# Staging tiles, the start of later attention and the order of the first loads in a fused attention, FFN and expert kernel

## The chip, the cores and the metric

The kernel runs on one core of one Trainium2 chip. Times are device microseconds of one launch, from the first to the last instruction and what lies around them. Engines are named as in the profile: PE (TensorE), DVE (VectorE), ACT (ScalarE), POOL (GpSimd), SP (SyncE, which here issues nearly all DMAs).

## What is computed

Three stages in a row, all in float32 at the interface:

```python
# 1. gated linear attention: 4 batches, 8 heads, 768 steps, head size 48
f = 1.0 / (1.0 + np.exp(-f_logit))
for t in range(S):
    state = f[:, :, t, :, None] * state + np.einsum('bhd,bhe->bhde', k[:, :, t], v[:, :, t])
    y[:, :, t] = np.einsum('bhd,bhde->bhe', q[:, :, t], state)
# 2. FFN over 3072 tokens: 384 -> 2048 -> 384
h = x @ w_in
x = (np.maximum(h, 0.0) + alpha * np.minimum(h, 0.0)) @ w_out
# 3. 8 experts with a capacity of 384 tokens each, filled greedily by the largest logit
logits = x @ w_gate
out[mask] = np.maximum(x[mask] @ w1[e], 0.0) @ w2[e]      # for each expert e
```

## The kernel before

The 3072 tokens are 24 chunks of 128; three chunks are a block, so there are eight blocks. Attention works chunk by chunk (`chunk`, steps `s1` to `s5`): `s1` runs two scans of 128x516 on DVE, a reciprocal and a minimum; `s2` multiplies keys and queries by the decays (two 128x512 products); `s3` makes scores on PE and masks them on DVE (two operations); `s4` and `s4s` make the output and the new state; `s5` halves the output into two parts for the FFN. All FFN matmuls have float32 operands, cut into a high and a low half, three matmuls in place of one.

The FFN weights come as pairs of 32-bit words (64-bit floats) and must be turned into such halves first: 16 chunks of 128 hidden columns, two chunks to a group `g`, eight groups. `load_w` issues four DMAs of a group (two of the first matrix, two of the second), `narrow` turns the words into floats (two ACT and two DVE instructions on 128x384 for each of 32 half chunks), `split` makes the halves (one ACT copy, one subtraction on DVE or POOL), and `gate` multiplies the second matrix by the gate on PE, so that logits come out of the FFN as eight more columns (three transposes, an ACT copy, three small matmuls, a small ACT copy and a small DVE subtraction per chunk). The result of `narrow` stands in a tile `a` of 128x384; there are three such buffers (lines 651, 666, 795, 805), so a new half chunk can be begun when an older one has been split and, for the second matrix, transposed for the gate.

`ffn1` runs one block: for each of 16 hidden chunks nine matmuls into one of two PSUM banks (`hidden`), a negative part, a combination on DVE (`SCALAR_TENSOR_TENSOR common`) and a split, and two chunks later nine matmuls into three output banks (`project`). At its end DVE copies the logits of the three chunks (`COPY lg`). In the traces and lists below, `MATMUL bank<-rounded,weights 128x384` is a hidden one and `bank<-weights,rounded 128x392` a projecting one; `weights14` and so on are the prepared weights, an even number for the first matrix of group 7, an odd one for the second.

The order of the work on each engine is made when the program is built: every operation is recorded with a priority, and `Plan.schedule` places them one by one, the one that by its costs can start first, ties by priority. It knows buffers, banks and dependencies; `behind(ops)` lets an operation start only after given ones have started. Where PE would stand idle and a bank is free, it puts in matmuls of ones (L1651). The engines then run these lists in order.

In `record`, the order around the change is: two chunk loads, attention of block 0, the weights (priority 15.5), then for b = 0 to 6 attention of block b+1 (priority 10b+10, 14 for block 1), and FFN of block b. The first loads on SP are chained by the string `FIRST` (c: a chunk's keys, queries, gates and values; w: a group of weights). A chunk's load is issued two chunks ahead into one of two buffers. `prepared` is the last operation of the weights; in the kernel before only the conversion of the expert weights (`convert`) waits for it.

Of the kernel before, what the change touches and what calls it, by code (L numbers as in the profile page):

```python
# [9 lines left out]
F32 = mybir.dt.float32  # L10
F32R = mybir.dt.float32r
BF = mybir.dt.bfloat16
I32 = mybir.dt.int32
# [7 lines left out]
N, DM, DF = B * S, H * D, 2048  # L21
# [8 lines left out]
KD = DM // 128  # L30
# [37 lines left out]
PLACES = 4  # L68
FILL = 2.0

FIRST = "c0 c1 w0 c2 w1 c3 w2 w3 c4 w4 w5 c5 w6 w7"
LOADS = 2


# [541 lines left out]
class Kernel:  # L616
# [28 lines left out]
    def constants(self, cp):  # L645
        nc = self.nc
        self.cp = cp
        self.ones = cp.tile([128, 128], BF, name="ones")
        with self.at(-4.0):
            nc.vector.memset(self.ones, 1.0)  # L650
        jp = self.sp.tile([128, 128], F32, name="a", bufs=3)
        nc.gpsimd.iota(jp, pattern=[[1, 128]], base=0, channel_multiplier=-1,
                       allow_small_or_imprecise_dtypes=True)
        self.ident = cp.tile([128, 128], F32, name="ident")
        nc.vector.tensor_scalar(self.ident, jp, 0.0, None, op0=OP.is_equal)
        self.mask = cp.tile([128, 128], BF, name="mask")
        nc.vector.tensor_scalar(self.mask, jp, 0.0, None, op0=OP.is_ge)
        self.tri = cp.tile([128, 128], BF, name="tri")
        nc.vector.tensor_scalar(self.tri, jp, 0.0, -1.0, op0=OP.is_le, op1=OP.mult)
        self.pick = cp.tile([2 * E, E], F32, name="pick")  # L660
        nc.vector.tensor_tensor(self.pick, self.ident[:2 * E, :E], self.ident[:2 * E, E:2 * E], OP.add)

        self.pairs = cp.tile([128, 128], F32, name="pairs")
        self.turn = cp.tile([128, 2], F32, name="turn")
        with self.at(PAIRS):
            two = self.sp.tile([128, 128], F32, name="a", bufs=3)
            nc.gpsimd.iota(two, pattern=[[2, 128]], base=0, channel_multiplier=-1, allow_small_or_imprecise_dtypes=True)
            nc.vector.tensor_scalar(self.pairs, two, 0.0, None, op0=OP.is_equal)
            nc.vector.tensor_reduce(self.turn[:, 0:1], self.pairs, axis=AX.X, op=OP.add)
            nc.vector.tensor_scalar(two, two, -1.0, None, op0=OP.is_equal)  # L670
            nc.vector.tensor_reduce(self.turn[:, 1:2], two, axis=AX.X, op=OP.add)
            nc.vector.tensor_add(self.pairs, self.pairs, two)
        self.eye8 = cp.tile([E, E], BF, name="eye8")
        nc.vector.tensor_copy(self.eye8, self.ident[:E, :E])

        self.cols = cp.tile([128, 128, 2], BF, name="cols")
        nc.gpsimd.iota(self.cols, pattern=[[1, 128], [0, 2]], base=0, channel_multiplier=0,
                       allow_small_or_imprecise_dtypes=True)
        nc.vector.tensor_scalar(self.cols, self.cols, -HALF, None, op0=OP.add)

        self.ok = cp.tile([WAYS + 1, 1], BF, name="ok1")
        nc.vector.memset(self.ok, -WAYS / 2.0)


        self.okl = cp.tile([WAYS + 2, E], BF, name="okl")
        nc.gpsimd.iota(self.okl[WAYS:], pattern=[[-1, E]], base=0, channel_multiplier=0, allow_small_or_imprecise_dtypes=True)
        nc.vector.tensor_scalar(self.okl[WAYS:], self.okl[WAYS:], 2.0 ** -13, None, op0=OP.mult)
        nc.vector.memset(self.okl[WAYS:WAYS + 1], -WAYS / 2.0 - 0.5)
        self.wts = cp.tile([128, E], F32, name="wts")
        nc.gpsimd.iota(self.wts, pattern=[[-1, E]], base=E, channel_multiplier=0,  # L690
                       allow_small_or_imprecise_dtypes=True)
        self.wtb = cp.tile([128, E], BF, name="wtb")
        nc.vector.tensor_copy(self.wtb, self.wts)
        self.jpv = cp.tile([128, NT, 2], F32, name="jpv")
        nc.gpsimd.iota(self.jpv[:, :, 0], pattern=[[1, NT]], base=0, channel_multiplier=0,
                       allow_small_or_imprecise_dtypes=True)
        nc.gpsimd.iota(self.jpv[:, :, 1], pattern=[[0, NT]], base=0, channel_multiplier=1,
                       allow_small_or_imprecise_dtypes=True)
        self.lg = cp.tile([128, NT, E], F32, name="lg")
        self.pmin = cp.tile([128, HP], F32, name="state")  # L700
        nc.vector.memset(self.pmin, 1.0)
# [89 lines left out]
    def prepare_in(self, g):  # L791

        a = []
        for u in range(2):
            a.append(self.sp.tile([128, KD, 128], I32, name="a", bufs=3))
            self.narrow(a[u], self.rin[:, u], self.nc.scalar)
        for u in range(2):
            f = 2 * g + u
            self.split(self.in_part(0, f), self.in_part(1, f), a[u].bitcast(F32))

    def prepare_out(self, g):

        a = []
        for u in range(2):
            a.append(self.sp.tile([128, DM], I32, name="a", bufs=3))
            self.narrow(a[u], self.rout[:, u], self.nc.scalar)
        for u in range(2):
            f = 2 * g + u
            self.split(self.out_part(0, f)[:, :DM], self.out_part(1, f)[:, :DM], a[u].bitcast(F32))
        for u in range(2):  # L810
            self.gate(2 * g + u, a[u].bitcast(F32))
# [846 lines left out]
    def record(self, cp):  # L1658
# [7 lines left out]
        def store(blk):  # L1666
            def put(t, r, logits):
                j = blk * BT + t
                (nc.sync if logits is not None else nc.scalar).dma_start(self.x2d[j * 128:(j + 1) * 128], r)
                if logits is not None:  # L1670
                    nc.vector.tensor_copy(self.lg[:, j, :], logits)
            return put
# [20 lines left out]
        def load(i):  # L1693
            self.load(i)
            loads["c", i] = self.last(3 if i else 5)

        def attend(b):
            with self.at(10.0 * b if b != 1 else ATT1):
                for i in range(b * BT, (b + 1) * BT):
                    self.chunk(i)  # L1700
                    if i + LOADS < NT:
                        with self.at(10.0 * b - 1):
                            load(i + LOADS)
# [17 lines left out]
        prepared = self.last(1)  # L1721
        self.slack = SLACK
        for b in range(NB - 1):
            attend(b + 1)
            if b == 0:
                steps = [loads[x[0], int(x[1:])] for x in FIRST.split()]
                self.plan.follow(steps)
            self.urgent = 10.0 * b + URG
            with self.at(10.0 * b + FFN):
                self.ffn1(self.xT.pop(b), store(b))  # L1730
# [95 lines left out]
```

## Time and profile before

| what | value |
| --- | --- |
| median of 3 runs | 872.51 us (870.24 to 876.36) |
| the profiled execution | 872.57 us |
| its span, first to last instruction | 870.6 us |
| PE busy | 829.7 us, 95% of the span |
| DVE busy | 580.2 us, 67% |
| ACT busy | 350.9 us, 40% |
| POOL busy | 118.6 us, 14% |
| mean granted TensorE clock | 0.979 |

The span falls into parts with different limits: up to about 147 us weights are prepared while attention and the FFN of the first block run; then FFN blocks and attention until about 534 us; then the choice of tokens and the eight experts. Shares of busy time over the whole span say little about the first part, so it is read by itself, in stretches and instruction by instruction. Busy PE time includes matmuls of ones and matmuls at the lower clock.

### The profile page before, as it was taken

To read this page: it belongs to the slowest core of one execution; us is meant where nothing else is said; L and a number is where in the kernel's file an instruction comes from. 1 tells how busy PE (TensorE), PEld (TensorE's weight loads), DVE (VectorE), ACT (ScalarE), POOL (GpSimd) and SP (SyncE) were. 2 spreads that over 40 slices of the span, in tenths; PEclk is the share of its full clock that TensorE was granted. 3 is DMA by queue.
4 is the path that set the end of the run, shared out by engine and by line. 5 is a ranking of instruction groups with operands and counts; after the bars stand their busy time and mean duration, and the time that the engine had idled before them with its cause. 6 is when DMAs were issued, how large, how long until landed. Compare 5 with 4: busy or idle time off the path is not lost. (4 is left out here: it accounts for less than half of the span.)

```text
span 870.6 us, 16049 instructions
## 1 busy us (share of the span) xinstructions
PE 829.7 (95%) x6125; PEld 764.4 (88%) x6125; DVE 580.2 (67%) x1302; ACT 350.9 (40%) x742; POOL 118.6 (14%) x111
## 2 busy tenths in 40 slices
PE   6999899999999999999999999998799999999995
PEld 4677788999999999999999998986688998999995
DVE  6998996956966966966976644655677568553220
ACT  3456775455455455455554433510112222212220
POOL 3100321200300200200300100000203203202211
PEclk7999998999999999999999999999899999999998
DMA  8996112888798698688778710007467865777400
GB/s 173 277 278 146 28 28 76 203 294 279 197 298 274 143 303 285 177 297 274 231 266 271 244 64 28 1 10 308 151 261 301 313 245 180 274 275 251 165 28 31
DMA packets 92790, 172.60 MB, mean 198 GB/s; under 512 B 31672, under 2 KB 61376, under 8 KB 92704
## 3 DMA queue, kind: packets, MB, share of 16 engines
q1 hardware_dynamic: 89056, 161.45, 58.3%
q0 software_dynamic: 3072, 9.44, 3.1%
q8 instruction: 50, 0.82, 0.4%
q10 hardware_dynamic: 576, 0.60, 0.2%
q14 instruction: 36, 0.29, 0.1%
HBM read 111.69 MB, written 59.77 MB: 197 GB/s over the span
## 5 line engine op out<-in xcount | busy, mean ns | idle before, releaser
L206 PE MATMUL bank<-rounded,weights 128*128 128x384 f32 (+1 forms) x1740 | 356.7, 346 | 2.8 <-POOL weights L206 1.6
L206 PE MATMUL bank<-weights,rounded 128*128 128x392 f32 (+1 forms) x1620 | 326.7, 346 | 3.5 <-DVE weights L206 1.9
L206 PEld LDWEIGHTS bank<-rounded,weights 128*128 128x128 f32 (+1 forms) x1740 | 306.0, 189 | 10.6 <-issue 3.7
L206 PEld LDWEIGHTS bank<-weights,rounded 128*128 128x128 f32 x1620 | 289.0, 189 | 6.9 <-DVE weights L206 3.3
L206 ACT ACTIVATE rounded<-bank 128x384 fp32r<-128x384 f32 x110 | 53.8, 491 | 198.1 <-PE bank L206 188.3
L206 DVE TENSOR_TENSOR early<-early 128x384 fp32r<-128x384 f32 (+2 forms) x196 | 117.5, 621 | 18.2 <-ACT early L206 17.0
L206 PEld LDWEIGHTS bank<-early 128*64 128x64 f32 (+2 forms) x1696 | 99.0, 154 | 19.1 <-issue 9.2
L206 PE MATMUL bank<-early 128*64 128x128 f32 (+3 forms) x1696 | 111.7, 271 | 1.0 <-ACT early L206 0.5
L206 DVE SCALAR_TENSOR_TENSOR common<-common,rest,bank 128x384 f32<-128x384 f32 x128 | 77.9, 609 | 49.4 <-ACT common L226 48.9
L206 ACT ACTIVATE early<-early 128x384 fp32r<-128x384 f32 (+2 forms) x177 | 95.3, 546 | 37.1 <-DMA wd<-early 22.4
L206 POOL TENSOR_TENSOR rounded<-common,rounded 128x384 fp32r<-128x384 f32 x40 | 52.6, 1315 | 366.3 <-ACT rounded L206 308.5
L226 ACT ACTIVATE common<-bank 128x384 f32<-128x384 f32 x128 | 62.5, 488 | 83.1 <-PE bank L206 82.3
L206 ACT ACTIVATE rounded<-common 128x384 fp32r<-128x384 f32 x118 | 61.7, 523 | 65.7 <-DVE common L206 65.5
L206 DVE TENSOR_TENSOR_SCAN early<-early 128x516 f32<-128x516 f32 x48 | 64.2, 1337 | 2.3 <-ACT early L206 1.2
L206 DVE SCALAR_TENSOR_TENSOR rounded<-bank,rounded 128x384 fp32r<-128x384 f32 x62 | 34.3, 554 | 46.4 <-ACT rounded L206 44.0
L206 DVE TENSOR_TENSOR rounded<-common,rounded 128x384 fp32r<-128x384 f32 x78 | 44.3, 569 | 27.8 <-ACT rounded L206 22.5
L206 ACT ACTIVATE common<-bank 128x384 f32<-128x384 f32 x48 | 23.3, 491 | 72.8 <-PE bank L206 69.3
L206 POOL DMA_INDIRECT out_dram<-common,late x24 | 25.5, 1062 | 171.3 <-ACT common L206 137.4
L206 POOL DMA_INDIRECT common<-x2d,late x24 | 26.8, 1118 | 150.8 <-DMA weights<-wd 119.5
L206 DVE TENSOR_TENSOR late<-late,cols 128x1536 bf16<-128x1536 bf16 (+3 forms) x53 | 42.7, 821 | 1.0
L206 DVE TENSOR_TENSOR early<-bank,mask 128x512 f32<-128x512 f32 x48 | 30.9, 684 | 6.1 <-PE bank L206 6.0
L206 DVE TENSOR_TENSOR rounded<-bank,rounded 128x384 fp32r<-128x384 f32 x48 | 26.3, 553 | 12.9 <-ACT rounded L206 12.4
(110 smaller groups left out, 494.8 us busy)
## 6 DMA issues: line engine op xcount, KB each, us to landing
wd<-early SPq DMA_DIRECT2D x128, 384.0 KB, 3.3
weights<-wd SPq DMA_DIRECT2D x64, 768.0 KB, 5.4
early<-in_w_dram SPq DMA_DIRECT2D x64, 384.0 KB, 4.3
early<-in_fkq_dram SPq DMA_DIRECT2D x46, 288.0 KB, 4.9
raw<-in_w_in_dram SPq DMA_DIRECT2D x16, 384.0 KB, 6.8
raw<-in_w_out_dram SPq DMA_DIRECT2D x16, 384.0 KB, 8.0
early<-in_v_dram SPq DMA_DIRECT2D x24, 192.0 KB, 4.9
x2d<-common SPq DMA_DIRECT2D x21, 192.0 KB, 3.0
```

The costliest lines, as they stand in the source:

```text
L206: op = self.add(engines, lambda e, b: getattr(e, method)(*[b(x) for x in a], **{n: b(x) for n, x in k.items()}), outs, ins)
L226: return e.activation(b(out), b(x), AF.Relu, scale=-1.0)
```

## The change

The staging tile `a` gets six buffers in place of three. Attention of blocks 2 to 7, with the chunk loads in it, starts only after the last operation of the weights has started (block 1 doesn't wait). The first loads stand in another order: w2, w4 and w6 go ahead of c3, c4 and c5.

```diff
-FIRST = "c0 c1 w0 c2 w1 c3 w2 w3 c4 w4 w5 c5 w6 w7"
+FIRST = "c0 c1 w0 c2 w1 w2 c3 w3 w4 c4 w5 w6 c5 w7"
+STAGE = 6
...
-        jp = self.sp.tile([128, 128], F32, name="a", bufs=3)
+        jp = self.sp.tile([128, 128], F32, name="a", bufs=STAGE)
...
-            a.append(self.sp.tile([128, KD, 128], I32, name="a", bufs=3))
+            a.append(self.sp.tile([128, KD, 128], I32, name="a", bufs=STAGE))
...
-            a.append(self.sp.tile([128, DM], I32, name="a", bufs=3))
+            a.append(self.sp.tile([128, DM], I32, name="a", bufs=STAGE))
...
         for b in range(NB - 1):
-            attend(b + 1)
+            with self.behind(prepared if b else ()):
+                attend(b + 1)
```

What this does to the lists of the engines is shown at three places.

DVE before, in the middle of the preparation, while groups 4 and 5 are narrowed (`raw_142`, `raw_138`, `raw_134`) and split (`weights_1042`, `weights_1081`). The rows `128x516` are scans, here of chunks 6 and 7, `state` is the minimum behind them.

```order
L206 SCALAR_TENSOR_TENSOR early<-raw_138,early 128x384
L206 TENSOR_TENSOR early<-early 128x512
L206 SCALAR_TENSOR_TENSOR common<-common,rest,bank_71 128x384
L206 TENSOR_TENSOR weights_1081<-early,weights_1081 128x384
L206 SCALAR_TENSOR_TENSOR early<-early,raw_134 128x384
L206 SCALAR_TENSOR_TENSOR early<-raw_134,early 128x384
L206 SCALAR_TENSOR_TENSOR common<-common,rest,bank_72 128x384
L206 SCALAR_TENSOR_TENSOR early<-early 128x516
L206 TENSOR_TENSOR weights_1081<-bank_65,weights_1081 128x2x8
L206 SCALAR_TENSOR_TENSOR early<-early,raw_134 128x384
```

DVE now, at the end of the FFN of block 0: the last gate subtractions (`weights_1276` is the second matrix of group 7), the logits, and right behind them the first scan of chunk 6.

```order
L207 TENSOR_TENSOR weights_1276<-bank_66,weights_1276 128x2x8
L207 TENSOR_TENSOR weights_1276<-bank_67,weights_1276 128x2x8
L207 COPY lg<-bank_68 128x8
L207 SCALAR_TENSOR_TENSOR early<-early 128x516
L207 COPY lg<-bank_69 128x8
L207 COPY lg<-bank_70 128x8
L207 RECIPROCAL early<-early 128x4
L207 SCALAR_TENSOR_TENSOR early<-early 128x516
L207 SCALAR_TENSOR_TENSOR common<-common,rest,bank_71 128x384
L207 TENSOR_TENSOR state<-state,early 128x4
L207 TENSOR_TENSOR early<-early 128x512 x2
```

Scans of chunks 6 to 9 (eight of them) stood ahead of the first logits before; now all stand behind. Up to the last split of `weights14`, DVE's list has lost six scans, four 128x512 products, three minima, three splits and some smaller rows.

PE before, from the first matmul on the first matrix of group 7 (`weights_1374`) on:

```order
L206 MATMUL bank_71<-rounded,weights_1374 128x384 x9
L206 MATMUL bank_72<-rounded,weights_1374 128x384 x9
L206 MATMUL bank_68<-weights_1310,rounded 128x392 x2
L206 MATMUL bank_69<-weights_1310,rounded 128x392 x3
L206 MATMUL bank_70<-weights_1310,rounded 128x392 x3
L206 MATMUL bank_67<-ident,early 128x128 x3
L206 MATMUL bank_65<-ident,early 128x128 x3
```

and now (`weights_1229` is the first matrix of group 7, `weights_1081` the second one of group 5):

```order
L207 MATMUL bank_71<-rounded,weights_1229 128x384 x9
L207 MATMUL bank_65<-early 128x8 x2
L207 MATMUL bank_72<-rounded,weights_1229 128x384 x9
L207 MATMUL bank_65<-early 128x8
L207 MATMUL bank_66<-ident,early 128x128
L207 MATMUL bank_67<-ident,early 128x128 x3
L207 MATMUL bank_68<-weights_1081,rounded 128x392
L207 MATMUL bank_69<-weights_1081,rounded 128x392
L207 MATMUL bank_70<-weights_1081,rounded 128x392
L207 MATMUL bank_66<-early 128x8
```

Before, 26 projecting matmuls were left of block 0 behind those 18 (8 on group 6, 18 on group 7); now it is 54 (18 on each of groups 5, 6 and 7). Counted to the last of them, PE has 72 big matmuls, 3 of the next block, 18 small gate matmuls and 13 transposes there. From the end of block 2's FFN on, PE's list is the same in both kernels but for five matmuls of ones; in all there are 100 of these before and 72 now, 69 and 42 of them up to the end of block 0's FFN.

## Rows read from the trace of the kernel before

**Rows 1.** The page, parts 1 and 2: PE's busy time, its slices and granted clock
```profile
PE 829.7 (95%) x6125; PEld 764.4 (88%) x6125; DVE 580.2 (67%) x1302; ACT 350.9 (40%) x742; POOL 118.6 (14%) x111
...
PEclk7999998999999999999999999999899999999998
```
**Rows 2.** Stretches from:to: length, busy us of each engine (instructions), clock, DMA share, GB/s
```profile
20.00:80.00 60.00, 55.55 (x513) 43.22 (x511) 55.74 (x105) 32.33 (x73) 5.99 (x6) 0.99 0.97 250
80.00:140.00 60.00, 55.36 (x344) 50.88 (x341) 54.29 (x99) 44.12 (x105) 13.69 (x12) 0.89 0.12 24
...
160.00:500.00 340.00, 340.00 (x2612) 326.64 (x2611) 253.05 (x451) 173.12 (x359) 34.18 (x25) 1.00 0.81 253
```
**Rows 3.** Groups by form on DVE, 20 to 147 us: count, busy us, mean ns, idle before
```profile
L206 DVE TENSOR_TENSOR_SCAN early<-early 128x516 f32<-128x516 f32 x17 | 23.2, 1366 | 0.5
L206 DVE SCALAR_TENSOR_TENSOR early<-early,raw 128x384 int32<-128x384 int32 x32 | 19.6, 613 | 2.0 <-ACT raw L206 2.0
L206 DVE SCALAR_TENSOR_TENSOR early<-raw,early 128x384 int32<-128x384 int32 x32 | 19.3, 603 | 0.7
L206 DVE TENSOR_TENSOR weights<-early,weights 128x384 fp32r<-128x384 f32 x26 | 14.8, 605 | 2.7 <-ACT weights L206 2.3
L206 DVE SCALAR_TENSOR_TENSOR common<-common,rest,bank 128x384 f32<-128x384 f32 x16 | 9.7, 604 | 2.3 <-ACT common L226 2.2
L206 DVE TENSOR_TENSOR early<-early 128x512 f32<-128x512 f32 x14 | 9.1, 682 | 0.0
L206 DVE TENSOR_TENSOR early<-bank,mask 128x512 f32<-128x512 f32 x10 | 6.4, 684 | 0.6 <-PE bank L206 0.6
L206 DVE TENSOR_TENSOR early<-early 128x384 f32<-128x384 f32 x6 | 3.6, 596 | 0.0
L206 DVE TENSOR_TENSOR early<-bank,early 64x192 f32<-64x192 f32 x10 | 3.5, 349 | 0.1
L206 DVE TENSOR_TENSOR rounded<-bank,rounded 128x384 fp32r<-128x384 f32 x6 | 3.3, 556 | 0.6 <-ACT rounded L206 0.5
...
L206 DVE TENSOR_TENSOR weights<-bank,weights 128x16 fp32r<-128x16 f32 x16 | 2.5, 166 | 2.1 <-ACT weights L206 2.0
...
L206 DVE TENSOR_TENSOR state<-state,early 128x4 f32<-128x4 f32 x9 | 2.2, 246 | 0.0
```
**Rows 4.** Timeline of DVE: start us, us, instruction, [idle before <-releaser]; splits of group 7, first logits
```profile
131.88 1.03 DVE L206 TENSOR_TENSOR weights<-early,weights 128x384 fp32r<-128x384 f32 x2
...
146.82 0.24 DVE L206 COPY lg<-bank 128x8 f32<-128x8 f32 x2 [1.70 <-ACT common L206]
```
**Rows 5.** Timeline of PE from group 7's first matrix to block 0's end
```profile
133.81 4.94 PE L206 MATMUL bank<-rounded,weights 128*128 128x384 f32 x18
...
141.65 1.18 PE L206 MATMUL bank<-early 128*128 128x8 f32 x10
...
145.27 1.88 PE L206 MATMUL bank<-weights,rounded 128*128 128x392 f32 x9
```
**Rows 6.** Timeline of PE at the end of block 2's attention
```profile
162.65 2.40 PE L206 MATMUL bank<-early 128*64 128x128 f32 x40
...
165.26 1.75 PE L206 MATMUL bank<-rounded,weights 128*128 128x384 f32 x9
166.86 1.78 PE L206 MATMUL bank<-weights,rounded 128*128 128x392 f32 x9
```
**Rows 7.** Timeline of POOL and DVE around 126 us: the same DVE operations twice
```profile
126.04 2.29 POOL L206 TENSOR_TENSOR rounded<-common,rounded 128x384 fp32r<-128x384 f32 x2 [7.84 <-PE bank L206]
...
126.21 1.25 DVE L206 SCALAR_TENSOR_TENSOR early<-early,raw 128x384 int32<-128x384 int32 x1
127.50 1.25 DVE L206 SCALAR_TENSOR_TENSOR early<-raw,early 128x384 int32<-128x384 int32 x1
...
130.08 0.55 DVE L206 SCALAR_TENSOR_TENSOR early<-early,raw 128x384 int32<-128x384 int32 x1
```
**Rows 8.** The densest stretch of ACT, columns as in rows 2
```profile
84.00:113.00 29.00, 26.11 (x145) 24.05 (x142) 27.48 (x49) 23.87 (x58) 8.17 (x6) 0.89 0.14 29
```

More of the change, by code (lines that the diff above doesn't have):

```diff
@@ L665, in constants @@
         with self.at(PAIRS):
-            two = self.sp.tile([128, 128], F32, name="a", bufs=3)
+            two = self.sp.tile([128, 128], F32, name="a", bufs=STAGE)
             nc.gpsimd.iota(two, pattern=[[2, 128]], base=0, channel_multiplier=-1, allow_small_or_imprecise_dtypes=True)
```

## The prediction

> **What bounds the kernel now.** I read the page first. PE is busy 95% of the span and its clock is near full in most slices [rows 1], so what counts is how much of PE's time is not useful work, and where. The stretches say where [rows 2]. From 160 to 500 us PE is busy without a gap at full clock: a change there can move work about but gains nothing. Before 140 us PE has gaps, matmuls of ones, and, from 80 to 140 us, a mean clock of 0.89, while DVE is busy 55.7 and 54.3 us of 60. So DVE sets the pace of the first part. The third view, DVE's groups by form between 20 and 147 us [rows 3], says with what: 64 narrowing operations (38.9 us), 17 scans (23.2), 26 splits (14.8). The idle times there are small and spread. DMA isn't what ends last: its share is 0.97 until 80 us and 0.12 after, so all first loads are in by about 80 us, while the weights of group 7 are split at 132 us [rows 4].
>
> At the end of this part the chain goes over to PE: behind group 7's split (ends 132.9 us) PE starts on that matrix at 133.8, and block 0's FFN ends at 147.1 (145.27 + 1.88); DVE, with nothing else, waits 1.7 us for the first logits at 146.8 [rows 4, 5]. The gain of the change, if any, is made before that point, kept or lost in block 1, and then carried to the end, since from block 2's end on PE's list is the same.
>
> **The buffers and the deferred attention, up to block 0's end.** Both take work out of DVE's way. By the lists, what stands ahead of the last split of group 7's first matrix falls by six scans (6 x 1.366 = 8.2 us), four products (4 x 0.682 = 2.7), three splits (1.8), three minima (0.7), four gate subtractions (0.7), two state additions (0.7), one state decay and one narrowing operation (0.6 each), and a few small ones, about 1 us together: 17.0 us by [rows 3]. Nothing of this is dropped; it stands later. If DVE is packed as before, that split ends at 132.9 - 17.0 = 115.9 us.
>
> But then PE is late. Before, 26 projecting matmuls of block 0 were left behind group 7's hidden ones; now 54 are, because group 7 is ready before PE has worked off groups 5 and 6. From group 7's first matmul PE has 75 big matmuls (9 take 1.60 us from start to start, so 0.178 each [rows 6]: 13.4 us), 18 small gate matmuls (ten records, two to a matmul, took 1.18 us [rows 5], so 0.236 each: 4.2) and 13 transposes (one record each, 0.118: 1.5), in all 19.1; I take 19.6 with small gaps. PE starts on group 7 at about 117, since nine projecting matmuls (1.6 us) stand between it and a gate subtraction that DVE does just ahead of the split. Block 0 then ends at 136.6 and the first logits are copied at 137 us in place of 146.8. DVE's 17 us have become 10, because PE is what is late next.
>
> The price from both sides: if PE were no limit there, DVE alone would end block 0 some 18 us earlier than now, about 129 us; if DVE packs worse, later. DVE and POOL show how: while POOL worked (126.04 to 128.33), two narrowing operations took 1.25 us each; the same one took 0.55 at 130.08 [rows 7]. That is 0.7 us for a collision. The list gives POOL two more weight splits before block 0's end and two FFN splits fewer, so I count no change here; if five or six more of them meet DVE, block 0 ends 4 us later, at 141. The Trainium skill (SBUF — State Buffer, section "SBUF: two separate sides") calls the port pair of the two engines an exclusive lock that the loser waits for during a whole instruction. By that rule a DVE list denser in operations with two SBUF inputs, as this one is, would lose more to the same number of POOL operations; the trace agrees in kind, with 1.25 against 0.55 us.
>
> ACT must keep up too: it is busy 23.9 of 29 us in its densest stretch [rows 8], and the list asks for no more than that between 40 and 117 us, so I count nothing for it.
>
> **The order of the first loads** moves one group of weights (four DMAs, 1.6 MB) ahead of chunks 3, 4 and 5, at some 250 GB/s [rows 2] about 6 us of delay for these chunks on SP's queue. I cost it at nothing: by DVE's new list the scans of chunk 3 stand some 10 us further back, behind the narrowing of group 1, and so hide it. If that cover were gone it would be up to 6 us on DVE in the first part, which has room of its own behind it, since PE is late at the end.
>
> **What the added wait does.** Attention of block 2 now begins behind the preparation, and in DVE's list its first scan stands right behind the first logits. FFN of block 1 doesn't need it, but PE's list has the scores, transposes and outputs of chunks 6, 7 and 8 between the first matmuls of block 1, so PE waits in order for DVE. Up to the second mask of chunk 8, DVE has 7 scans (9.6 us), 6 products (4.1), 6 masks (4.1), 4 FFN combinations (2.4), 2 decays (1.2), 2 halvings (1.1), 4 state operations (1.4), and small ones of 1.7: 25.6 us [rows 3]. Then PE makes chunk 8's outputs in 2.4 us [rows 6]. So that point comes at 137 + 25.6 + 2.4 = 165.0.
>
> Before, PE was through with chunk 8 at the same 165.0 (162.65 + 2.40), but by then had done 29 big matmuls of block 1 less (counted in the lists: 9 and 9 hidden ones, 10 and 1 projecting ones), 29 x 0.178 = 5.2 us. For equal work the points are 170.2 before and 165.0 after: a gain of 5.2 us. From there on DVE has about 34 us for some 41 us of PE, and PE bounds.
>
> From below, the wait costs nothing if PE is as late as DVE: PE alone needs 61 big matmuls (10.9 us), 76 scores and outputs (9.1, 0.12 each by the 20 of [rows 6]), 12 transposes and 24 small ones (some 2.8): 22.8 us, so 159.4 and a gain of 10.8. From above, DVE's chain is longer: each of three chunks adds its round trip to PE (eight scores, 0.9 us, and about 1 us of handing over) and seven POOL operations collide (0.7 each): 25.6 + 5.7 + 4.9 = 36.2 us, so 175.6 and a loss of 5.4. I take 25.6, the sum nearest to rows of DVE where it was packed like this.
>
> The sum: 872.57 us of the profiled execution (span 870.6) less 5.2 is 867.4. The median of the three runs, 872.51, is the same to 0.1.
>
> **The rivals.**
>
> *The deferred attention hides behind PE.* PE in block 1 is so late that DVE's chain costs nothing: 872.57 - 10.8 = 861.8 us. For it: consecutive operations on DVE overlap a little, so a packed list may run faster than its sum. Against it: DVE starts on block 2's first scan only at the first logits.
>
> *The preparation is no faster.* DVE and ACT, both nearly full, wait for each other more, or POOL's collisions grow; block 0 ends at 141 and 1.2 us are left: 871.4. For it: ACT's dense stretch [rows 8]. Against it: idle times on DVE are small [rows 3]. The clock is a lesser form: 18 matmuls of group 7 took 4.94 us [rows 5] in place of 3.2, at the lower level of 1.2 GHz; before that PE had waited for DVE. The same once more between 117 and 137 costs 1.7 us. The Trainium skill (TensorE: Matmul & The Clock Gate, section "What's actually happening") says that the default is the throttled state and activity releases it; by that rule 27 fewer matmuls of ones before block 0's end speak against the change, though 0.89 was granted with all of them in.
>
> *Slower: the deferred attention becomes block 1's bound.* One place, chunks 6 to 8 behind the first logits; its price is the 36.2 us above: 872.57 + 5.4 = 878.0. It decides from a chain of 31 us on (170.2 - 137 - 2.4 = 30.8). For it: all of block 2's DVE work, formerly spread over 60 us, now stands in one row. Against it: no engine but DVE is full there.
>
> **How the numbers follow.** Forecast (864 to 870 us) 0.45; hidden attention (861.8, 859 to 864) 0.25; no faster preparation (871.4, 870 to 874) 0.18; longer chain (878.0, 874 and above) 0.12. One per cent is 8.7 us, about what a measurement of this kernel can tell from no change: below 863.8 lies the second case and a little of the first, 0.27; above 881.3 the tail of the last, 0.05; the rest, 0.68, between. The range from 860 to 875 leaves out about a tenth at the top, less below.
>
> **What would show it.** Right: the first logits at 135 to 139 us; group 7's split some 15 us earlier and PE later than it; PE waiting for DVE's masks several times between 140 and 163 us; chunk 8's outputs ending near 165; the same distance in time from the end of block 2 on. Wrong: PE's wait on masks missing (then 862), group 7's split later than 120 us (then 871), or a chain from first logits to chunk 8's last mask of more than 31 us (then slower).

## The result and the profile after

Over eight runs each the changed kernel took 865.98 us (median; 863.8 to 867.32) against 873.34 us (870.24 to 876.36): ratio 0.9911, 95% interval 0.9893 to 0.993. Of the single executions that were profiled, 872.57 us became 866.27 us (span 864.0), 6.3 us less. Forecast: 867.4 us, a gain of 5.2 us.

The page of after, parts 1 and 2, answers to [rows 1]. PE's share of the span is the same 95% of a shorter span; behind the first slice (0.8 in place of 0.7) the clock has one slice at 0.8 in the first part as before, the fifth in place of the seventh.

```profile
PE 821.9 (95%) x6097; PEld 760.4 (88%) x6097; DVE 577.9 (67%) x1299; ACT 350.5 (41%) x742; POOL 123.6 (14%) x114
...
PEclk8999899999999999999999999999899999999998
```

The stretches, in the columns of [rows 2]. DVE has 43.8 us of work left between 80 and 140 us where it had 54.3, PE's time from 160 to 500 us is as full as it was:

```profile
20.00:80.00 60.00, 53.96 (x477) 46.10 (x475) 57.49 (x105) 38.94 (x88) 15.48 (x13) 0.94 0.88 237
80.00:140.00 60.00, 55.67 (x384) 51.89 (x379) 43.76 (x89) 37.16 (x92) 7.97 (x7) 0.94 0.15 41
...
160.00:500.00 340.00, 340.00 (x2600) 326.36 (x2601) 253.36 (x454) 171.88 (x357) 37.66 (x26) 1.00 0.79 248
```

DVE's groups by form from 20 us to the first logits (136 us), as [rows 3] (one of the two narrowing groups is shown): narrowing is all there, of 17 scans only 9 are left. DVE now waits ahead of splits (2.5 us in all), gate subtractions (4.7) and, most of all, five FFN splits (6.5) that stand between them.

```profile
L207 DVE SCALAR_TENSOR_TENSOR early<-raw,early 128x384 int32<-128x384 int32 x32 | 19.4, 607 | 0.7
...
L207 DVE TENSOR_TENSOR weights<-early,weights 128x384 fp32r<-128x384 f32 x24 | 13.9, 597 | 2.5 <-ACT weights L207 1.9
L207 DVE TENSOR_TENSOR_SCAN early<-early 128x516 f32<-128x516 f32 x9 | 12.5, 1386 | 0.4 <-ACT early L207 0.2
...
L207 DVE TENSOR_TENSOR rounded<-common,rounded 128x384 fp32r<-128x384 f32 x5 | 3.5, 706 | 6.5 <-issue 2.2 <-ACT weights L207 2.1 <-ACT rounded L207 2.0
...
L207 DVE TENSOR_TENSOR weights<-bank,weights 128x16 fp32r<-128x16 f32 x16 | 2.6, 168 | 4.7 <-ACT weights L207 4.6
```

DVE's timeline, as [rows 4]: the two splits of group 7's first matrix, the last gate subtraction, the first logits, the first scan of chunk 6, one scan beside POOL, and the masks of chunk 8.

```profile
115.10 1.02 DVE L207 TENSOR_TENSOR weights<-early,weights 128x384 fp32r<-128x384 f32 x2
...
135.28 0.18 DVE L207 TENSOR_TENSOR weights<-bank,weights 128x16 fp32r<-128x16 f32 x1 [2.12 <-ACT weights L207]
136.25 0.17 DVE L207 COPY lg<-bank 128x8 f32<-128x8 f32 x1 [0.79 <-PE bank L207]
136.47 1.23 DVE L207 TENSOR_TENSOR_SCAN early<-early 128x516 f32<-128x516 f32 x1
...
145.92 2.08 DVE L207 TENSOR_TENSOR_SCAN early<-early 128x516 f32<-128x516 f32 x1
...
159.60 1.26 DVE L207 TENSOR_TENSOR early<-bank,mask 128x512 f32<-128x512 f32 x2
```

And PE's timeline, as [rows 5, 6]: group 7's first matrix, the last projecting matmuls of block 0, the only two waits that are marked in chunks 6 to 8 (both for transposes), a single hidden matmul ahead of scores, and chunk 8's outputs.

```profile
116.81 1.75 PE L207 MATMUL bank<-rounded,weights 128*128 128x384 f32 x9
...
135.51 1.78 PE L207 MATMUL bank<-weights,rounded 128*128 128x392 f32 x9
...
149.32 0.66 PE L207 MATMUL bank<-ident,early 128*128 128x128 f32 x4 [0.16 <-DVE early L207]
149.73 0.42 PE L207 MATMUL bank<-rounded,weights 128*128 128x384 f32 x1
150.08 1.76 PE L207 MATMUL bank<-early 64*128 64x128 f32 x32
...
156.94 0.66 PE L207 MATMUL bank<-ident,early 128*128 128x128 f32 x4 [0.23 <-DVE early L207]
...
160.90 2.40 PE L207 MATMUL bank<-early 128*64 128x128 f32 x40
163.23 1.71 PE L207 MATMUL bank<-weights,rounded 128*128 128x392 f32 x8
```

So the split ends at 116.12 us (132.91 before), the first logits come at 136.25 (146.82), and chunk 8's outputs end at 163.3. From the first logits of block 1 (202.9 after, 209.2 before) to those of block 7 (566.5, 572.8) the two traces stay 6.3 to 6.5 us apart: nearly all of it is gained up to the end of block 1.

**Where the time came from.** PE's time up to that point is real work, matmuls of ones, or nothing. The stretches give PE's busy time, and the stretches of the ones alone what of it was filler. Before (the columns of [rows 2]; first the stretches, then the ones alone; the stretch from 20 to 80 us stands in [rows 2]):

```profile
80.00:146.80 66.80, 62.16 (x404) 57.22 (x401) 57.36 (x105) 46.37 (x111) 16.45 (x13) 0.90 0.14 34
146.80:209.20 62.40, 62.34 (x448) 59.43 (x448) 44.95 (x80) 31.27 (x65) 5.04 (x4) 1.00 0.83 246
...
20.00:80.00 60.00, 10.06 (x38) 0.99 0.97 250
80.00:146.80 66.80, 3.26 (x12) 0.90 0.14 34
```

After:

```profile
80.00:136.20 56.20, 51.87 (x363) 48.41 (x359) 40.18 (x80) 34.10 (x85) 7.97 (x7) 0.94 0.14 33
136.20:202.90 66.70, 66.31 (x503) 62.40 (x502) 55.65 (x96) 33.81 (x69) 10.11 (x7) 1.00 0.65 179
...
136.20:163.20 27.00, 26.61 (x280) 22.73 (x278) 25.86 (x45) 14.02 (x28) 5.39 (x5) 1.00 0.48 103
...
20.00:80.00 60.00, 5.75 (x20) 0.94 0.88 237
80.00:136.20 56.20, 0.81 (x3) 0.94 0.14 33
```

Idle time and ones together: from 20 to 80 us 14.5 before (60 - 55.55 + 10.06) and 11.8 after (60 - 53.96 + 5.75); from 80 us to the first logits 7.9 and 5.1; in block 1 0.1 and 0.4. With the first 20 us, 14.1 in both, that is 36.6 against 31.5: 5.1 us of the 6.3 were empty PE time that real work now fills, 2.7 of them between 20 and 80 us, which the prediction's sum doesn't have. The other 1.2 us are real work done in less time: 172.6 us of PE before, 171.4 after. Two later profiles of the changed kernel (in the table below) have 30.9 and 31.1 us of empty time, but 170.3 and 168.7 us of real work at clocks of 0.94 and 0.95. So the empty time is the steady part of the gain, and in these three profiles the time of the real work moves with the clock.

Block 1 itself became longer, 66.7 us in place of 62.4. PE's groups by form say with what. Before, from 146.8 to 209.2 us:

```profile
L206 PE MATMUL bank<-weights,rounded 128*128 128x392 f32 x141 | 28.0, 342 | 0.0
...
L206 PE MATMUL bank<-ident,early 128*128 128x128 f32 x4 | 0.7, 286 | 0.0
L206 PE MATMUL bank<-early 128*64 128x48 f32 x16 | 0.6, 220 | 0.0
```

After, from 136.2 to 202.9 us:

```profile
L207 PE MATMUL bank<-weights,rounded 128*128 128x392 f32 x150 | 30.4, 344 | 0.0
...
...
L207 PE MATMUL bank<-early 128*64 128x48 f32 x48 | 2.0, 226 | 0.0
L207 PE MATMUL bank<-ident,early 128*128 128x128 f32 x12 | 1.9, 282 | 0.4 <-DVE early L207 0.4
```

Nine more projecting matmuls (1.6 us at 0.178) lie between the two logits: five of block 0 that are now done behind its first logits, and four of block 1 that are now done ahead of its own. The transposes of two chunks (1.2) and the 32 records of their small matmuls of 128x48 (1.4) used to stand ahead of the first logits and now stand behind, and 0.4 us are a wait (two hidden matmuls of block 1 moved ahead). That is why 10.6 us at the first logits are 6.3 at the end of block 1: most of the difference is work moved, not time lost.

### The profile page after: what moved, and what is told of

The parts are those of the page before. It is cut to its first block, busy times and chain, and to the rows that moved or that the text cites. A ratio compares the mean times of both kernels' runs of the same rounds, so it can differ in the third digit from the quotient of the medians.

```text
span 864.0 us, 15985 instructions
## 1 busy us (share of the span) xinstructions
PE 821.9 (95%) x6097; PEld 760.4 (88%) x6097; DVE 577.9 (67%) x1299; ACT 350.5 (41%) x742; POOL 123.6 (14%) x114
## 5 line engine op out<-in xcount | busy, mean ns | idle before, releaser
L207 PEld LDWEIGHTS bank<-rounded,weights 128*128 128x128 f32 (+1 forms) x1740 | 302.8, 188 | 9.8 <-issue 3.7
L207 PEld LDWEIGHTS bank<-early 128*64 128x64 f32 (+2 forms) x1696 | 102.0, 157 | 16.7 <-issue 7.7
L207 POOL TENSOR_TENSOR rounded<-common,rounded 128x384 fp32r<-128x384 f32 x41 | 56.3, 1372 | 374.0 <-ACT rounded L207 344.0
L207 DVE TENSOR_TENSOR rounded<-common,rounded 128x384 fp32r<-128x384 f32 x77 | 43.8, 569 | 32.4 <-ACT rounded L207 22.2
L207 DVE SCALAR_TENSOR_TENSOR rounded<-bank,rounded 128x384 fp32r<-128x384 f32 x62 | 34.3, 554 | 46.5 <-ACT rounded L207 45.0
```

Of the source, the lines that this page charges most:

```text
L207: op = self.add(engines, lambda e, b: getattr(e, method)(*[b(x) for x in a], **{n: b(x) for n, x in k.items()}), outs, ins)
```

## The experiments

Three jobs on three chips, each with its own runs of the kernel before beside it: 871.05 us (29 runs), 873.98 (22) and 871.33 (11), in the table's order from "six buffers alone", "after, 2nd" and "after, 3rd" on. Medians compare within a job; the ratio is an estimate of its own, not the quotient of the medians. Diffs are against the changed kernel. The milestones come from single traces and are starts of instructions (the split itself takes some 0.5 us more); "empty" is PE idle time and ones up to block 1's first logits, worked out as above; the clock is the one granted up to the first logits.

| kernel | median us | ratio to before (95%) | last split of group 7's first matrix | first logits | block 1's logits | empty | clock |
| --- | --- | --- | --- | --- | --- | --- | --- |
| before | 873.34 | 1 | 132.4 | 146.8 | 209.2 | 36.6 | 0.92 |
| after | 865.98 | 0.9911 (0.9893–0.993) | 115.6 | 136.2 | 202.9 | 31.5 | 0.92 |
| six buffers alone | 865.72 | 0.9948 (0.9921–0.9974) | 118.9 | 140.2 | 203.0 | 32.9 | 0.95 |
| wait alone | 866.6 | 0.9965 (0.9943–0.9986) | 127.9 | 138.3 | 203.5 | 33.4 | 0.94 |
| loads alone | 865.17 | 0.9934 (0.9913–0.9955) | 126.9 | 139.2 | 202.3 | 32.2 | 0.98 |
| buffers and wait, 1st | 863.03 | 0.9927 (0.9902–0.9953) | 115.3 | 134.4 | 199.8 | 30.9 | 0.95 |
| after, 2nd | 864.77 | 0.9892 (0.9861–0.9922) | 113.8 | 134.5 | 201.2 | 30.9 | 0.94 |
| buffers and loads | 870.32 | 0.9956 (0.9935–0.9976) | 117.8 | 142.3 | 205.8 | 34.8 | 0.93 |
| wait for splits only | 867.14 | 0.9908 (0.9879–0.9937) | 115.7 | 139.4 | 204.0 | 35.3 | 0.94 |
| after without ones | 876.65 | 1.002 (1.0–1.0041) | 118.9 | 140.6 | 206.2 | 30.2 | 0.94 |
| after, 3rd | 862.86 | 0.9909 (0.9884–0.9933) | 112.9 | 133.6 | 199.8 | 31.1 | 0.95 |
| buffers and wait, 2nd | 862.12 | 0.9899 (0.9863–0.9936) | 116.8 | 135.9 | 201.3 | 32.7 | 0.95 |
| wait and loads | 863.46 | 0.9909 (0.9887–0.9931) | 124.8 | 137.5 | 202.4 | 34.7 | 0.96 |
| four buffers | 865.58 | 0.9933 (0.9906–0.996) | 122.7 | 139.2 | 203.5 | 34.3 | 0.96 |

**Each part alone.** Six buffers alone:

```diff
-FIRST = "c0 c1 w0 c2 w1 w2 c3 w3 w4 c4 w5 w6 c5 w7"
+FIRST = "c0 c1 w0 c2 w1 c3 w2 w3 c4 w4 w5 c5 w6 w7"
-            with self.behind(prepared if b else ()):
+            with self.behind(()):
```

> Six buffers alone, old order of loads, no wait. Theory (DVE's list sets group 7's split, PE's list then block 0's end): DVE's list up to that split falls by 8.7 us against the kernel before (125.0 in place of 133.7 by its durations), PE has 15.0 us from there, but DVE's list up to the first logits is nearly the old one (141.1 in place of 141.6), so the first logits come at 143 to 146 us (146.8 before) and the time is 0 to 4 us below the kernel before. Rival (the buffers are what gains, the wait only moves work): first logits at 136 to 138 us and the whole gain of 7 us.

The wait alone (the old `FIRST`, and):

```diff
-STAGE = 6
+STAGE = 3
```

> The wait alone, three buffers, old order of loads. Theory: group 7's split by DVE's list at 123.3 - 0.8 = 122.5 us, PE has 10.9 us from there, first logits at about 134 to 137 us; then the deferred attention (26.1 us of DVE) sets chunk 8's outputs to end near 163 to 166, as in the changed kernel; gain 5 to 7 us. Rival (with three buffers DVE can't be fed, so it idles where attention stood): group 7's split later than 128 us, first logits later than 141, and, as the deferred attention still follows, no gain or a loss of up to 3 us.

The loads alone (`STAGE = 3` and `self.behind(())`):

> The order of the first loads alone. Theory (costed at nothing in the prediction): within 2.5 us of the kernel before; DVE's list up to the first logits is 139.3 us long in place of 141.6, so first logits at 144 to 147. Rival (the loads are what lets the weights be ready early): first logits before 141 us and a gain of 5 us or more.

Measured: 5.3, 4.5 and 5.9 us less than the 871.05 beside them, with intervals that overlap. By the ratios they make 0.52, 0.35 and 0.66%, 1.5% together, where the whole change made 0.9 to 1.1% in its three jobs; so the parts don't add up. Without the wait, buffers and loads together (0.9956) make no more than either alone.

The buffers and the wait came out between their theories and their rivals: first logits at 140.2 us, earlier than the 143 to 146 of the first theory, and group 7's split at 127.9, later than the 122.5 of the second, with 4.5 us in place of 5 to 7. What surprised was the loads, which the prediction had costed at nothing: their theory fell and the rival held. The split of group 7 comes 5.5 us earlier and the first logits 7.6 us. The stretches of that kernel:

```profile
20.00:80.00 60.00, 52.89 (x493) 43.96 (x491) 55.74 (x101) 36.48 (x82) 13.44 (x11) 1.00 0.86 241
80.00:140.00 60.00, 54.28 (x373) 48.45 (x372) 54.05 (x104) 42.27 (x103) 13.58 (x11) 1.00 0.21 47
```

DVE is as busy as in [rows 2], so it wasn't given less to do; but ACT gets 36.5 us done before 80 us (32.3 before) and POOL 13.4 (6.0): halves of the weights are made earlier and PE finds work in place of ones (empty time 32.2 against 36.6). That the weights are there earlier is what the edit asks for; no row here shows it apart. The clock is 1.00 in both stretches where it was 0.99 and 0.89, and over all runs 0.986 in the mean against 0.982: by the 5.0 us for 0.01 of the last section, some 2 of the 5.9 us go with the clock.

An open end: every edit makes the planner order all lists anew, and no run tries an edit that should do nothing. How much of a part's 4 to 6 us is the part, and how much the order that the planner happened on, isn't shown.

**Two of three.** Buffers and wait (the first loads in the old order), once beside the parts and once beside the whole change:

```diff
-FIRST = "c0 c1 w0 c2 w1 w2 c3 w3 w4 c4 w5 w6 c5 w7"
+FIRST = "c0 c1 w0 c2 w1 c3 w2 w3 c4 w4 w5 c5 w6 w7"
```

> The change without the new order of loads (six buffers and the wait). Theory: group 7's split at 118.0 - 0.8 = 117 us, PE 18.8 us from there, first logits at 136 to 139; the time within 2 us of the changed kernel. Rival (the loads carry part of the gain): first logits later than 140, and 3 us or more of the gain lost.

> Six buffers and the wait, with the first loads in the old order, now beside the whole change. Theory: with the wait in place the scans that the new order would push back are gone from the preparation anyway, so the order adds nothing: within 1.5 us of the whole change. Rival: the new order, which brings chunks 3 to 5 later, costs time here: the old order is 2 us or more faster (863.0 against 866.0 and 864.8, on different chips, point that way), and the first logits come 1 us or more earlier with it.

> The changed kernel again, as the reference for the three runs beside it. Both theories expect 863 to 867 us and the first logits at 134 to 137 us, as in its two earlier profiles (136.2 and 134.5).

862.12 against 862.86 us in the same job (the whole change itself came out a little below what was expected of it): no difference, and the first logits 2.3 us later rather than earlier, so the rival fell. Beside the other two parts the order of loads is worth nothing that shows; the six runs of the old order spread over 8 us, so 2 or 3 us could hide.

Wait and loads, without the buffers (`STAGE = 3`), and the whole change with four of them (`STAGE = 4`):

> The wait and the new order of loads with three buffers as before: the whole change without its buffers. Theory: with two of the three parts in, block 0's end is set by PE and not by the preparation, so three buffers do: by the list DVE's work up to the last split of group 7's first matrix is 4.6 us more than in the whole change (split at about 120 us), but PE has 12.5 us in place of 18.8 left behind it, so the first logits come at 133 to 136 us and the time is within 2 us of the whole change. Rival: the buffers carry the gain, since ACT and DVE wait for each other's tiles with three of them: the split comes at 124 us or later and the time is 3 us or more above the whole change.

> The whole change with four staging buffers in place of six. Theory: as for three buffers, block 0's end is set by PE: split at about 119 us, 15.4 us of PE left behind it in place of 18.8, the first logits at 134 to 137 us, time within 2 us of the whole change. Rival: each buffer shortens the preparation and the end with it: 1.5 us or more slower than the whole change, with the split and the first logits later by as much.

With three buffers 863.46 us: 0.6 us from the whole change, as the theory had it. Its split comes 11.9 us later than in the whole change, at 124.8 us, and its first logits only 3.9 us later (DVE's timeline; there is less of PE's work left behind the split):

```profile
124.36 1.03 DVE L207 TENSOR_TENSOR weights<-early,weights 128x384 fp32r<-128x384 f32 x2 [0.65 <-ACT weights L207]
...
136.56 0.17 DVE L207 TENSOR_TENSOR weights<-bank,weights 128x16 fp32r<-128x16 f32 x1 [2.56 <-ACT weights L207]
137.51 0.17 DVE L207 COPY lg<-bank 128x8 f32<-128x8 f32 x1 [0.78 <-PE bank L207]
```

The split was past the rival's mark of 124 us and the first logits past the theory's 136, yet the medians didn't follow: by them, where the preparation ends decides little here. The traces don't settle it, since with three buffers block 7's first logits come 2.2 us later (565.6 against 563.4) and half of that is made up behind them. Four buffers came out 2.7 us above the whole change, more than the theory's 2 us and in the size that the rival gave, with intervals that overlap. As three do better, the number alone doesn't explain it; whether the order that the planner found with four does, stays open.

Buffers and loads, without the wait, beside the whole change:

```diff
-            with self.behind(prepared if b else ()):
+            with self.behind(()):
```

> The change without the wait (six buffers and the new order of loads). Theory (the wait's price is paid in block 1, where DVE does the deferred attention in a row): group 7's split near 117.6, first logits at 135 to 138 as in the changed kernel, since PE's 17 us from group 7 on set them; DVE's list from there to chunk 8's last mask is 17.6 us in place of 26.1, so block 1 takes 62 to 64 us (66.7 in the changed kernel) and the time is 3 to 4 us below the changed kernel. Rival (the wait is what clears DVE's way): first logits later than 140 us and the time 2 us or more above the changed kernel.

> The changed kernel again, beside the next three: 864 to 867 us, first logits near 136 us, logits of block 1 near 203.

870.32 against 864.77 us: 5.5 us slower, so the theory that the wait costs some microseconds fell and its rival held. DVE's timeline without the wait:

```profile
117.33 1.01 DVE L207 TENSOR_TENSOR weights<-early,weights 128x384 fp32r<-128x384 f32 x2
...
124.89 0.79 DVE L207 TENSOR_TENSOR weights<-early,weights 128x384 fp32r<-128x384 f32 x1
...
125.81 1.23 DVE L207 TENSOR_TENSOR_SCAN early<-early 128x516 f32<-128x516 f32 x1
...
127.46 0.17 DVE L207 TENSOR_TENSOR weights<-bank,weights 128x16 fp32r<-128x16 f32 x1
...
140.47 0.17 DVE L207 TENSOR_TENSOR weights<-bank,weights 128x16 fp32r<-128x16 f32 x1 [2.83 <-ACT weights L207]
```

and PE's:

```profile
127.68 1.34 PE L207 MATMUL bank<-weights,rounded 128*128 128x392 f32 x6 [1.58 <-DVE weights L207]
129.84 3.23 PE L207 MATMUL bank<-weights,rounded 128*128 128x392 f32 x9 [0.81 <-ACT weights L207]
```

Scans of block 2 stand between the splits and gate subtractions of group 7; PE waits 1.58 us for DVE there, for the subtraction behind a scan, and 0.81 for ACT, and its next nine matmuls run at the lower clock (3.23 us where nine take 1.78; granted clock 0.52 from 129.8 to 133.0 us). So read, the wait's benefit is that this late-needed work can't stand in front of work that PE is about to need.

The wait for the splits alone, not the gate:

```diff
             self.split(self.out_part(0, f)[:, :DM], self.out_part(1, f)[:, :DM], a[u].bitcast(F32))
+        self.halved = self.last(1)
...
-            with self.behind(prepared if b else ()):
+            with self.behind(self.halved if b else ()):
```

> The change with an earlier end of the wait: attention of block 2 waits for the last split of the weights, not for the last gate subtraction behind it. Theory (between them DVE waits some 2 us for each of six gate results while PE works off groups 5 to 7, so three chunks of scans fit in there at no cost): first logits within 1.5 us of the changed kernel's 136, block 1 in 62 to 64 us in place of 66.7, the time 3 to 4 us below the changed kernel. Rival (scans of 1.3 us in front of the gate subtractions hold up PE's projecting matmuls): first logits 3 us or more later and no gain against the changed kernel.

Block 1 became 2.1 us shorter (64.6 us), but the first logits came at 139.4, 4.9 us later than in the run of the whole change beside it: 2.4 us slower by the medians, with intervals that overlap, so there was no gain and the rival held. Again scans stand in front of small gate subtractions, here up to the last one:

```profile
135.55 1.23 DVE L207 TENSOR_TENSOR_SCAN early<-early 128x516 f32<-128x516 f32 x1
...
137.50 0.17 DVE L207 TENSOR_TENSOR weights<-bank,weights 128x16 fp32r<-128x16 f32 x1 [0.66 <-ACT weights L207]
```

**The matmuls of ones.** The whole change without them:

```diff
-                plan.filler = lambda e, k: e.matmul(banks[k], self.ones, idle, start=True, stop=True)
+                plan.filler = None
```

> The changed kernel without any matmuls of ones, for what the clock is worth in the first part. Theory (DVE sets the pace up to group 7's split, PE only behind it): the granted clock of 20 to 80 and 80 to 140 us falls from 0.94 each to below 0.85; group 7's split comes at most 4 us later, and block 0's end 3 to 8 us later, because PE's 19 us behind the split run in part at the lower level. Rival (the clock doesn't matter there): first logits within 1.5 us of 136. Rival (the ones themselves delay useful matmuls): first logits earlier than 135.

11.9 us slower than with them. Two stretches without them, in the first part and where the experts begin (35.4 us behind block 7's first logits; 35.2 in the other kernel):

```profile
20.00:60.00 40.00, 33.07 (x276) 30.84 (x273) 37.32 (x71) 26.21 (x62) 9.74 (x8) 0.83 0.98 265
...
608.00:668.00 60.00, 51.04 (x346) 43.60 (x347) 35.39 (x125) 9.33 (x19) 9.95 (x10) 0.72 0.61 237
```

and the same two of the whole change beside it:

```profile
20.00:60.00 40.00, 34.95 (x345) 28.04 (x342) 38.45 (x71) 22.61 (x50) 7.34 (x6) 0.98 0.98 268
...
600.00:660.00 60.00, 52.93 (x433) 43.59 (x431) 42.50 (x144) 11.79 (x24) 12.11 (x11) 0.97 0.63 248
```

Empty time up to block 1's logits is not more (30.2 us), but these logits come 5.0 us later, since the real work takes 176.0 us of PE in place of 170.3. In the two stretches the clock is lower while PE has real work, 0.83 against 0.98 and later 0.72 against 0.97. The theory had the clock below 0.85 from 20 to 80 and from 80 to 140 us, and that fell: it was 0.89 and 0.97 (0.96 and 0.97 with the ones), and the mean up to the first logits is 0.94 in both kernels. So that the clock makes all of the 5.7 us is not shown. The first logits, 6.1 us later, are in the theory's range, the split, 5.1 us later, a little outside. Over all runs the clock was 0.969 in the mean (10 runs) against 0.984 (6). The planner also orders the rest otherwise where it has no ones to place; that part wasn't taken apart.

## Why the prediction came out right

- **DVE's list up to group 7's split** (17.0 us less, split ends at 115.9): measured 116.12. The term is right, but that it fits to 0.2 us is luck: a second and a third profile of the same kernel put the split 1.8 and 2.7 us earlier.
- **PE is late next** (starts at 117, first logits at 137 in place of 146.8): it started at 116.81 and the logits came at 136.25. The rows show which engine waits: DVE stands idle 2.1 us ahead of the last gate subtraction, at the end of a chain (transposes, copy, small matmuls, copy) that passes through PE twice.
- **Loads at nothing**: right inside the whole change as far as the medians tell (862.12 against 862.86), but the reason given was too narrow. It asked only what the delay of chunks 3 to 5 costs, not what earlier weights give; alone they give 5.9 us.
- **The added wait**: 25.6 us of DVE from the first logits to chunk 8's last mask, outputs' end at 165.0. Measured 24.6 us (160.86 - 136.25) and 163.3. DVE was packed as the sum supposed (one scan beside POOL took 2.08 us, another 1.23), the longer chain of 36.2 us didn't come. But the sign named for it, PE waiting for masks, is missing: two waits of 0.16 and 0.23 us, for transposes. The prediction read that absence as the hidden case of 861.8 us, and that was wrong: its bound gave PE 22.8 us of work there, while PE was busy 26.6 of 27.0 us. Some 0.9 us of these are block 0's last projecting matmuls, which run on behind the first logits. The rest, 25.7 us counted from start to start, is what the sum had at 22.8: scores, outputs, small matmuls and transposes took 12.7 us (11.9 in the sum), and the 61 big matmuls 13.0 in place of 10.9, at 0.213 us each where the sum took 0.178 from unbroken rows of nine. Between short groups they cost more: the single one at 149.73 holds PE for 0.35 us, until the scores start at 150.08. So PE's work and DVE's list came out equally long and neither waited; that DVE's sum alone gave the time is in part luck.
- **The sum**: 5.2 us predicted, 6.3 in the profiled executions, 7.4 by the medians (6.1 to 9.3 by the interval). The term that was mis-sized is that point in block 1, 1.7 us too late; from there to block 1's logits 0.6 us of it were lost. What the medians show beyond 6.3 can lie in the clock, below.

On POOL's collisions with DVE, POOL's timeline beside the scan of 2.08 us shown above:

```profile
145.91 1.00 POOL L207 TENSOR_TENSOR rounded<-common,rounded 128x384 fp32r<-128x384 f32 x1 [2.00 <-ACT rounded L207]
```

The scan that began 0.01 us behind POOL's operation took 2.08 us in place of 1.23. It is some 0.9 us for one collision; [rows 7] had 0.7 for another operation. By the Trainium skill (SBUF — State Buffer, section "SBUF: two separate sides") the loser of the port pair waits; the trace agrees, with these 0.9 us.

On the clock: the 28 matmuls of ones that went cost nothing that shows. In the job of the second profile the mean clock was 0.984 (6 runs) against 0.982 before (22 runs), and up to the first logits it was 0.92 in both kernels of the first pair of profiles. Taking out all of them cost 11.9 us. By the Trainium skill (TensorE: Matmul & The Clock Gate, section "What's actually happening") the default state is throttled and activity releases the throttle. The run without ones agrees, with a granted clock of 0.83 from 20 to 60 us; what the prediction made of the rule for this change did not come: here real work took the place of the ones.

## What to carry to other kernels

When several edits speed up the same stretch, ask what is late next before adding their gains: here each of three gained 0.35 to 0.66%, all three together 0.9 to 1.1%, and two with the wait among them as much as all, as far as the runs tell. Count a gain as empty time of the engine that bounds the span (idle time and filler) that disappears, up to a point behind which the lists agree; a milestone such as the first logits overstates it by whatever work was moved behind it. Empty time alone doesn't rank the kernels, though: buffers and loads and wait and loads have 34.8 and 34.7 us of it, and ratios of 0.9956 and 0.9909. How long the real work took (171.0 and 167.7 us of PE) has to be read beside it. Work that is needed late should be held back from an engine's list while another engine needs short operations on it: the kernels in which scans of 1.2 us stood in front of gate subtractions of 0.17 us were 5.5 and 2.4 us slower.

## What was not expected

Single executions differ by more than some edits do, and the clock differs with them. Over the 22 runs of the kernel before in the second job, time and mean granted clock go together (correlation -0.83; 5.0 us less for 0.01 more), and three profiles of the changed kernel, whose lists are the same, have their first logits at 136.2, 134.5 and 133.6 us with clocks of 0.92, 0.94 and 0.95 up to there. Milestones of two single traces therefore compare to some 2 or 3 us only, and small differences between the variants are read from medians. And no variant came below 30 us of empty PE time up to block 1, some 14 of it in the first 20 us.
